# A schedule searched anew: halved first loads, wide filler matmuls and another list of steps

## The chip, the cores and the metric

The kernel runs on one core of a Trainium2 chip. Its time is the device time of one execution in microseconds. Three runs of the kernel before took 821.39, 821.52 and 822.88 us, so the median is 821.52 us; the profiled execution took 821.7 us. The engines are TensorE (PE, with PEld for its weight loads), VectorE (DVE), ScalarE (ACT), GpSimd (POOL) and SyncE (SP), which issues most transfers.

## The reference, cut to what matters

Three stages follow one another on 2304 tokens (4 sequences of 576) with 512 features (8 heads of 64):

```python
kv  = einsum('bhsd,bhse->bhde', k, v)          # linear attention, per batch and head 64x64
out = einsum('bhsd,bhde->bhse', q, kv)
out = out / sqrt(mean(out*out, -1) + 1e-6) * g_norm      # per head
x   = out as (2304, 512)
xn  = x / sqrt(mean(x*x, -1) + 1e-6) * rms_g
x   = (silu(xn @ w_gate) * (xn @ w_val)) @ w_out         # 512 -> 1536 -> 512
h   = x @ w_in
out = where(h > 0, h, exp(min(h, 0)) - 1) @ w_out2       # 512 -> 2048 -> 512
```

The weights arrive in 64 bits and are turned into 32-bit numbers on the chip.

## The kernel before, in words

The tokens lie in 18 tiles of 128. A batch of 576 tokens is four and a half tiles, so tile 4 is shared by batches 0 and 1, and tile 13 by batches 2 and 3. For each batch `sum_kv` (L933) adds up the products of k and v over its tiles in one PSUM bank (step `kv`), `keep_kv` (L954) copies the sum to SBUF on ACT (`kept`), and `attend` (L972) multiplies the queries of a tile with it (`po`). The queries of two tiles come in one load (q0 for tiles 0 and 1, q1 for 2 and 3, q2 for 4 and 5). Behind `po` stand, for every tile, a square on ACT, a mean and a guard on DVE, a power on POOL, two multiplications on DVE, a second square on ACT, a power on POOL and a scaling on ACT (`norm2`). `turn` (`pt`, L1036) transposes two tiles on PE, and ACT and DVE split the result into two parts, xh and xl (L1048, L1046).

The feed-forward stages multiply in three products of such parts (high by high, high by low, low by high). Each weight block has to be converted first (`conversion`, L1079): about six steps on DVE and two on ACT give a high part `h_` and a low part `l_`. The names g0, v0, o0 are the first blocks of w_gate, w_val and w_out; i and p are those of the last stage. Block 0 of tokens (tiles 0 and 1) is multiplied first: `hid_0_0` needs xh and xl of these tiles and g0 and v0; `b_0_0` and `b_0_1` need the gated result (`act`) and o0. Partial sums of the second products are copied to SBUF by ACT (`part`) and added in memory by transfers from POOL.

What stands where is written out in advance. Every piece of work is a step with an engine, an assumed length, predecessors and the buffers it takes. The method `order` (L77) chooses the buffers by a greedy pass over ranks that a table SHIFTS alters; the table ORDER then gives the order in which the instructions of all engines are written. Loads go through SP in one queue. Where the list expects PE to wait between two steps, `run` (L154) puts in filler matmuls of 128 columns (`keep_warm`, L925); they write to an unused part of the bank of the running `kv` sum, so outside such a sum there are none. Ahead of everything PE runs 14 matmuls of 128 columns on zeros (`idle`, L876). Both kinds are in 32-bit floats, and the trace shows two records for one such matmul of 128 columns.

Of the kernel before, what the change touches and what calls it, by code (L numbers as in the profile page):

```python
# [20 lines left out]
WARM = 16  # L21
# [3 lines left out]
class Plan:  # L25
# [6 lines left out]
    PATIENCE = 0.03  # L32
# [25 lines left out]
    def lag(self, e, engine):  # L58
        return self.LAG[e][0] if e == engine else self.LAG[e][1] + self.into.get(engine, 0.0)

    def room(self, kind, engine, chosen):

        best = None
        for slot in self.kinds[kind]:
            if slot in chosen:
                continue
            key = self.holder.get(slot)
            at = 0.0
            if key is not None:
                if any(u not in self.ends for u in self.users[key]):  # L70
                    continue
                at = max((self.reach(u, engine) for u in self.users[key]), default=0.0)
            if best is None or at < best[0]:
                best = at, slot
        return best

    def order(self):  # L77
        self.holder, self.where = dict(self.held), {}
        self.ends, self.log, self.rooms = {}, [], []
        self.clock = dict(self.start)  # L80
        waits = {n: len(s["after"]) for n, s in self.steps.items()}
        ready = {e: [] for e in self.clock}
        for n, k in waits.items():
            if not k:
                ready[self.steps[n]["engine"]].append((n, 0.0))
        left = len(self.steps)
        while left:
            best = None
            for engine, names in ready.items():
                now = self.clock[engine]  # L90
                here = None
                for n, at in names:
                    s = self.steps[n]
                    at = max(now, at)
                    if here and at > here[0] + self.PATIENCE:
                        continue
                    slots = []
                    for kind, key in s["takes"]:
                        r = self.room(kind, engine, [x for x, _ in slots])
                        if r is None:  # L100
                            break
                        at = max(at, r[0])
                        slots.append((r[1], key))
                    if len(slots) < len(s["takes"]):
                        continue
                    if here is None or at < here[0] - self.PATIENCE or (
                        at <= here[0] + self.PATIENCE and (s["rank"], at) < (here[1], here[0])
                    ):
                        here = at, s["rank"], n, slots
                if here and (best is None or here[:2] < best[:2]):  # L110
                    best = here
            if best is None:
                return None
            at, _, n, slots = best
            s = self.steps[n]
            engine = s["engine"]
            for slot, key in slots:
                if slot in self.holder:
                    self.rooms.append((self.holder[slot], n))
                self.holder[slot] = key  # L120
                self.where[key] = slot
            ready[engine] = [x for x in ready[engine] if x[0] != n]
            self.ends[n] = at + s["length"] + s["lat"]
            self.clock[engine] = at + s["length"]
            self.log.append((at, n, engine, s["length"]))
            for x in self.then.get(n, ()):
                waits[x] -= 1
                if not waits[x]:
                    e = self.steps[x]["engine"]
                    ready[e].append((x, max(self.reach(y, e) for y in self.steps[x]["after"])))  # L130
            left -= 1
        return max(self.ends.values())

    def timed(self):

        after = {n: list(s["after"]) for n, s in self.steps.items()}
        for key, taker in self.rooms:
            after[taker] += self.users[key]
        names = list(self.steps)
        assert sorted(ORDER) == list(range(len(names)))  # L140
        self.ends, self.log = {}, []
        self.clock = dict(self.start)
        for i in ORDER:
            n = names[i]
            s = self.steps[n]
            engine = s["engine"]
            at = max([self.clock[engine] if engine != "NOTE" else 0.0] + [self.reach(x, engine) for x in after[n]])
            self.ends[n] = at + s["length"] + s["lat"]
            self.clock[engine] = at + s["length"]
            self.log.append((at, n, engine, s["length"]))  # L150
# [3 lines left out]
    def run(self):  # L154
        self.held, self.start = dict(self.holder), dict(self.clock)
        self.then = {}
        for n, s in self.steps.items():
            for x in s["after"]:
                assert x in self.steps, (n, x)
                self.then.setdefault(x, []).append(n)  # L160
        for n, s in self.steps.items():
            unit = str(n[0] if isinstance(n[0], tuple) else n[:4]).replace(" ", "")
            s["rank"] += SHIFTS.get(unit, 0)
        self.into = {}
        assert self.order(), "no step can start"
        self.into = self.INTO
        self.timed()
        last, end = 0.0, self.steps[self.filled_until]
        for at, n, e, length in self.log:
            call = self.steps[n]["call"]  # L170
            if e == "PE":
                if call and end and last:
                    for _ in range(int((at - last - self.SPACE) / self.FILL)):
                        self.filler()
                last = at + length
                end = end if n != self.filled_until else None
            if call:
                call()


SHIFTS = {
# [625 lines left out]
def linear_attention__swiglu__elu_kernel(  # L807
# [341 lines left out]
    def load(n):  # L1149
        raw_sb[n] = stage(weight[n].bitcast(U32), ("raw", n))  # L1150
# [1034 lines left out]
```

## Time and profile before

| what | value |
|---|---|
| median of three runs | 821.52 us (821.39 to 822.88) |
| profiled execution | 821.7 us, span 819.9 us, so 1.8 us lie around the span |
| mean granted TensorE clock | 0.996 |
| PE, DVE, ACT, POOL busy | 99%, 91%, 78%, 28% |
| memory traffic | 57.2 MB read, 66.1 MB written |

The span runs from the first to the last instruction. An idle time of PE is only seen where no matmul runs; the views used below are the engines' busy time by stretch with the granted clock (1.00 is 2.4 GHz, 0.50 is 1.2 GHz), the waits, and the instructions in order of time.

### The profile page before, as it was taken

Reading aid. Unit: us, or ns where it says so; the run is one execution under the profiler, and the core shown is the slowest. Engines: PE = TensorE matmul, PEld = TensorE weight load, DVE = VectorE, ACT = ScalarE, POOL = GpSimd, SP = SyncE. Lnnn points to the kernel's source line nnn. Section 1 sums busy time; section 2 is a strip of 40 time slices with the busy share of each in tenths; the row PEclk is TensorE's granted clock in tenths of the full one; section 3 lists DMA queues with packets and bytes.
Section 4 is the critical chain, followed back from the end, with each engine's and each line's share of the span. In section 5 each row is a group of like instructions: output and inputs, shape, how many; then the busy total and the mean of one; then the engine's idle time right before and its main releaser. Section 6 shows DMA issues by size and latency. Waiting matters only on the chain.

```text
span 819.9 us, 12523 instructions
## 1 busy us (share of the span) xinstructions
PE 809.4 (99%) x4228; PEld 683.8 (83%) x4228; DVE 747.7 (91%) x1360; ACT 636.7 (78%) x1209; POOL 230.8 (28%) x258
## 2 busy tenths in 40 slices
PE   8999999999999999999999999999999999999997
PEld 7888888888888888888888888888888888888886
DVE  3999999998787888888999999999999999999895
ACT  2789777777677676667655789999999999999891
POOL 3556222123223213113300000123333334233332
PEclk9899999999999999999999999999999999999999
DMA  9953468558657748648972242789989998989989
GB/s 363 354 172 101 119 124 164 125 104 150 132 104 141 131 100 138 121 91 136 159 193 78 78 151 87 183 129 145 158 161 174 155 170 137 182 154 141 124 176 249
DMA packets 56144, 124.06 MB, mean 151 GB/s; under 512 B 6160, under 2 KB 10000, under 8 KB 56080
## 3 DMA queue, kind: packets, MB, share of 16 engines
q0 software_dynamic: 30944, 54.01, 47.4%
q1 hardware_dynamic: 25136, 69.25, 24.6%
q8 instruction: 33, 0.54, 0.3%
q14 instruction: 31, 0.25, 0.1%
HBM read 57.18 MB, written 66.06 MB: 150 GB/s over the span
## 4 chain that ended last, share of the span: by engine, by line
PE 97%; DMA 2%; SPq 0%; DVE 0%; issue 0%
PE b L1362 11%; PE hid L1520 7%; PE hid_g L1520 3%; PE hid_v L1520 3%; PE b L1347 2%; PE po L981 2%; DMA wacc<-in_q 1%; PE pt L1036 1%; DMA wxl<-in_q 1%; PE kv L943 1%; PE ('pu', 0, 10, 3)_a L1231 1%; PE ('pu', 0, 4, 1)_a L1231 1%; PE ('pb', 10, 1)_a L1699 1%; PE ('pu', 0, 11, 3)_a L1231 1%; PE ('pu', 0, 7, 3)_a L1231 1%; PE ('pb', 4, 3)_a L1699 1%
## 5 line engine op out<-in xcount | busy, mean ns | idle before, releaser
L1756 POOL DMA_DIRECT2D out<-part x104 | 91.8, 910 | 163.4 <-DVE part L1723 62.7
L1756 POOL DMA_DIRECT2D mid<-part x64 | 57.0, 1037 | 187.4 <-ACT part L1733 79.9
L1428 ACT ACTIVATE part<-b 128x512 f32<-128x512 f32 x66 | 38.9, 596 | 10.5 <-PE b L1362 3.9
L1434 POOL DMA_DIRECT2D out<-part x12 | 11.0, 917 | 125.4 <-DMA out<-part 107.7
L1565 ACT ACTIVATE e<-e 128x512 f32<-128x512 f32 (+1 forms) x73 | 45.1, 625 | 0.9
L1434 POOL DMA_DIRECT2D mid<-part x26 | 27.7, 1152 | 59.1 <-ACT part L1428 57.0
L1362 PE MATMUL b<-act,h_o 128*128 128x512 f32 x128 | 39.7, 392 | 0.0
L1663 DVE TENSOR_TENSOR e<-e,e 128x512 f32<-128x512 f32 x56 | 38.4, 686 | 0.5
L1001 POOL TENSOR_TENSOR ri<-ms,nhalf 128x8 f32<-128x8 f32 x18 | 32.7, 1818 | 11.8 <-DVE ms L997 11.7
L1362 PEld LDWEIGHTS b<-act,h_o 128*128 128x128 f32 x128 | 23.6, 188 | 4.8 <-issue 0.2
L1362 PE MATMUL b<-act,l_o 128*128 128x512 f32 x64 | 24.9, 389 | 0.0
L1362 PE MATMUL b<-h_p,act 128*128 128x512 f32 (+1 forms) x68 | 23.1, 378 | 0.5 <-DVE far L1468 0.5
L1487 DVE TENSOR_TENSOR far<-far,b 128x512 f32<-128x512 f32 x27 | 18.0, 683 | 5.3 <-PE b L1362 5.1
L1362 PE MATMUL b<-act,h_p 128*128 128x512 f32 x64 | 19.8, 390 | 0.0
L1048 ACT ACTIVATE xh<-pt,gains_sb 128x256 fp32r<-128x256 f32 x36 | 15.7, 480 | 3.8 <-PE pt L1036 3.8
L1347 PE MATMUL b<-act,h_o 128*128 128x256 f32 x96 | 18.2, 285 | 0.0
L1520 PE MATMUL hid<-xh,l_i 128*128 128x256 f32 x64 | 18.1, 283 | 0.0
L1520 PE MATMUL hid<-xl,h_i 128*128 128x256 f32 x64 | 18.1, 283 | 0.0
L1520 PE MATMUL hid<-xh,h_i 128*128 128x256 f32 x64 | 17.9, 280 | 0.0
L1347 PEld LDWEIGHTS b<-act,h_o 128*128 128x128 f32 x96 | 15.9, 190 | 1.3
L1046 DVE SCALAR_TENSOR_TENSOR xl<-pt,gains_sb,xh 128x256 fp32r<-128x256 f32 x36 | 15.9, 476 | 1.1 <-ACT xh L1048 1.1
L1019 POOL TENSOR_TENSOR ri<-ms,nhalf 128x1 f32<-128x1 f32 x18 | 11.0, 615 | 19.0 <-ACT junk L1015 18.9
(2362 smaller groups left out, 3183.8 us busy)
## 6 DMA issues: line engine op xcount, KB each, us to landing
out<-part POOLq DMA_DIRECT2D x116, 256.0 KB, 5.3
mid<-part POOLq DMA_DIRECT2D x90, 256.0 KB, 5.4
raw_i<-in_w_in SPq DMA_DIRECT2D x16, 512.0 KB, 5.0
raw_p<-in_w_out SPq DMA_DIRECT2D x16, 512.0 KB, 5.5
raw_g<-in_w_gate SPq DMA_DIRECT2D x12, 512.0 KB, 5.4
raw_v<-in_w_val SPq DMA_DIRECT2D x12, 512.0 KB, 4.5
raw_o<-in_w_out SPq DMA_DIRECT2D x12, 512.0 KB, 4.8
mid<-part SPq DMA_DIRECT2D x18, 256.0 KB, 2.2
```

What stands on the lines that cost most here:

```text
L981: nc.tensor.matmul(po[r:r1, p * P:(p + 1) * P], qt[:, p, r:r1], kv_sb[b][:, p, :], start=True, stop=True)
L1001: nc.gpsimd.tensor_tensor(ri, ms_t.pop(i), nhalf, op=ALU.pow)
L1231: nc.tensor.matmul(pbank[unit, b], l[:, sl], r, start=first and c == 0 and i == 0, stop=c == 1 and i == 2, skip_group_check=True,)
L1347: nc.tensor.matmul(po[:, j * n:(j + 1) * n], l[:, s], r, start=first and i == j == 0, stop=f == fs[-1] and i == 2, skip_group_check=True,)
L1362: nc.tensor.matmul(po, l, r, start=first and i == 0 and not half, stop=f == fs[-1] and i == 2, skip_group_check=seeded(ph, k, t) or half i ...
L1428: nc.scalar.activation(x, pbank["b", k, t, e][:, :n], AF.Copy)
L1434: nc.gpsimd.dma_start(out=where(ph, t, e), in_=flat(live.pop(key), t or ph), accum_op=ALU.add)
L1487: nc.vector.tensor_tensor(x, x, pbank["b", k, t, e][:, :n], op=ALU.add)
L1520: nc.tensor.matmul(pbank[key][:, j * n:(j + 1) * n], l, r, start=bool(opens) and i == 0, stop=c == KD - 1 and i == 2, skip_group_check=not ...
L1565: nc.scalar.activation(live[key], live[key], AF.Exp, scale=-1.0)
L1663: nc.vector.tensor_tensor(raw(*into), raw(*x), raw(*y), op=ALU.subtract)
L1756: lambda key=key, t=t, e=e: nc.gpsimd.dma_start(out=where(ph, t, e), in_=live.pop(key), accum_op=ALU.add),
```

## The change

1. **Shared tile and first queries in halves.** Tile 4 is packed on the host so that the half of batch 0 (`4a`) and that of batch 1 (`4b`) are each 512 columns over all 128 partitions, and each is a load of its own. q0 is loaded as `q0a` and `q0b`, one for each of its tiles.
2. **Loads reordered.** SP issued 0, 1, 2, 3, 4, q0, gains, g0, q1, 5, 6, 7, 8, v0, q2, o0, q3, q4, 9 and now issues 0, 1, 2, 3, 4a, g0, gains, q0a, q0b, q1, v0, 6, 4b, 5, 7, 8, q2, o0, 9, q3, 10, 12, 11, 13, 16, 14, 15, g1, q4, 17, q5.
3. **Fillers.** One filler matmul has up to 512 columns; where no `kv` sum is open it writes to the bank that the step behind it will take. The matmuls on zeros at the start are 5 of 512 columns.
4. **List searched anew.** SHIFTS and the greedy pass are gone; ORDER and a new table PLACES (the buffer for each take) are written out. The assumed times of the loads and of PE's start differ, and the steps `whole` wait for both of the last tiles' powers.

```diff
-WARM = 16
+WARM = 5
...
-                    for _ in range(int((at - last - self.SPACE) / self.FILL)):
-                        self.filler()
+                    self.filler(n, int((at - last - self.SPACE) / self.FILL))
...
-SHIFTS = {
-    "('go',0)": -166, "('in',0)": -1299, "('go',1)": -9, "('in',1)": -385, "('go',2)": 8, "('in',4)": 28,
...
+PLACES = (
...
-WHOLE_AFTER = 17
+WHOLE_AFTER = 16, 17
...
-    for j in range(WARM - 2):
-        nc.tensor.matmul(idle[:, :P], blank, blank, start=True, stop=True)
+    for j in range(WARM):
+        nc.tensor.matmul(idle, blank, blank.unsqueeze(1).to_broadcast([P, 4, P]), start=True, stop=True)
...
-    def load_kv_tile(i):
-        in_sb[i] = home(i)
-        nc.sync.dma_start(out=in_sb[i], in_=kv[i].rearrange("t j e -> t (j e)"))
+    def load_kv_tile(i, part=None):
+        if i not in in_sb:
+            in_sb[i] = home(i)
+        cs = slice(0, 2 * DM) if part is None else slice(part * DM, (part + 1) * DM)
+        nc.sync.dma_start(out=in_sb[i][:, cs], in_=kv[i][:, cs])
...
-    def keep_warm():
-        if spot:
-            nc.tensor.matmul(spot[0], ident, ident, start=False, stop=False, skip_group_check=True)
+    def keep_warm(n, times):
+        taken = [key for _, key in plan.steps[n]["takes"]]
+        if times > 0 and not spot and taken:
+            own = ps.tile([P, 512], F32, tag=plan.where[taken[0]], name="_".join(map(str, ("warm", *n))))
+        most = 2 if spot else 4
+        while times > 0 and (spot or taken):
+            k = min(times, most)
+            wide = ident.unsqueeze(1).to_broadcast([P, k, P])
+            if spot:
+                nc.tensor.matmul(spot[0][:, :k * P], ident, wide, start=False, stop=False, skip_group_check=True)
+            else:
+                nc.tensor.matmul(own[:, :k * P], ident, wide, start=True, stop=True)
+            times -= k
...
+            if packed:
+                r0 = h % 2 * D
+                r1 = r0 + D
+                at = part * DM + h // 2 * D
+                to = at + HALF
...
-    LOADS = [0, 1, 2, 3, 4, 'q0', 'gains', 'g0', 'q1', 5, 6, 7, 8, 'v0', 'q2', 'o0', 'q3', 'q4', 9, 10, 11, 12, 13, 'q5', 'q6', 14, 15, 16, 17, 'g1', 'v1', 'q7', 'o1', 'q8']
+    LOADS = [0, 1, 2, 3, '4a', 'q0a', 'q0b', 'gains', 'g0', '4b', 'q1', 5, 6, 7, 8, 'v0', 'q2', 'o0', 'q3', 'q4', 9, 10, 11, 12, 13, 'q5', 'q6', 14, 15, 16, 17, 'g1', 'v1', 'q7', 'o1', 'q8']
...
-    plan.clock["DMA"], plan.clock["PE"] = 3.85, 6.75
+    plan.clock["DMA"], plan.clock["PE"] = 2.5, 6.1
...
+    cut = s // P
+    cut_rows = arrays["kv"][cut].reshape(2, d, 2, h // 2, 2, d)
+    arrays["kv"][cut] = cut_rows.transpose(4, 1, 0, 2, 3, 5).reshape(P, 2 * dm)
```

On PE, from the last products of batch 0 to the queries of tile 4 (`po_297` before, `po_308` after), this stood before; `wxl` and `wacc` are the buffers of the loaded tiles and queries, and `kv_105` is the kept sum of batch 0:

```order
L943 MATMUL kv_116<-wacc_142 64x64 x8
L981 MATMUL po_170<-kv_105,wxl_153 128x128 x4
L981 MATMUL po_179<-kv_105,wxl_153 128x128 x4
L943 MATMUL kv_191<-wacc_142 64x64 x8
L981 MATMUL po_200<-kv_105,wacc_175 128x128 x4
L981 MATMUL po_215<-kv_105,wacc_175 128x128 x4
L943 MATMUL kv_191<-wacc_188 64x64 x16
L943 MATMUL kv_191<-wacc_224 64x64 x8
L927 MATMUL kv_191<-ident 128x128
L943 MATMUL kv_191<-wacc_224 64x64 x8
L981 MATMUL po_297<-kv_105,wacc_175 64x128 x4
L981 MATMUL po_297<-kv_106,wacc_175 64x128 x4
```

Before there is one filler here, and none directly ahead of the queries of tile 4. Now the same engine has, from behind the queries of tile 3 (`po_201`) to those of tile 4:

```order
L537 MATMUL warm_kv_4_224<-ident 128x512
L537 MATMUL warm_kv_4_224<-ident 128x128
L562 MATMUL kv_227<-wacc_134 64x64 x8
L535 MATMUL kv_227<-ident 128x256
L535 MATMUL kv_227<-ident 128x128
L562 MATMUL kv_227<-wacc_206 64x64 x16
L562 MATMUL kv_227<-wacc_238 64x64 x8
L535 MATMUL kv_227<-ident 128x128
L562 MATMUL kv_227<-wacc_238 64x64 x8
L537 MATMUL warm_po_306<-ident 128x512
L602 MATMUL po_308<-kv_96,wacc_174 64x128 x4
L602 MATMUL po_308<-kv_97,wacc_174 64x128 x4
```

The products of tile 4 for batch 1 moved behind the queries of tiles 2 and 3, and fillers of 1664 columns in all stand here, 512 of them directly ahead of the queries of tile 4.

On DVE, at the place where o0 becomes ready for `b_0_0` (`l_o` is its low part, `act` the gated result), this stood before:

```order
L1115 TENSOR_SCALAR c_o_351<-raw_o_288 128x512
L1544 TENSOR_TENSOR sa_0_424<-sa_0_424,hid_0_0_362 128x256
L1118 ISA w_o_399<-w_o_399,c_o_351 128x1024
L997 TENSOR_SCALAR ms_411<-ms_411 128x8
L994 TENSOR_REDUCE ms_472<-z_67 128x8
L1305 TENSOR_TENSOR act_0_0_0_431<-sa_0_424,act_0_0_0_431 128x256
L1004 TENSOR_TENSOR z_71<-po_297,ri_422 128x512
L1127 SCALAR_TENSOR_TENSOR l_o_477<-w_o_399,h_o_458 128x512
```

And this stands there now:

```order
L736 TENSOR_SCALAR c_o_323<-raw_o_296 128x512
L618 TENSOR_SCALAR ms_393<-ms_393 128x8
L739 ISA w_o_409<-w_o_409,c_o_323 128x1024
L618 TENSOR_SCALAR ms_422<-ms_422 128x8
L1165 TENSOR_TENSOR sa_0_436<-sa_0_436,hid_0_0_385 128x256
L625 TENSOR_TENSOR z_71<-po_308,ri_414 128x512
L748 SCALAR_TENSOR_TENSOR l_o_471<-w_o_409,h_o_451 128x512
L926 TENSOR_TENSOR act_0_0_0_473<-sa_0_436,act_0_0_0_473 128x256
```

From the first step of g0 to the last row here DVE has the same steps in both lists, but for one guard more after the change; within the list, g0's six steps now come before the first mean, and `l_v`, the low part of v0, before the first `xl`.

## Rows read from the trace of the kernel before

**Rows 1.** The page, part 1: busy us (share of the span) xinstructions of each engine.

```profile
PE 809.4 (99%) x4228; PEld 683.8 (83%) x4228; DVE 747.7 (91%) x1360; ACT 636.7 (78%) x1209; POOL 230.8 (28%) x258
```

**Rows 2.** Stretches: us, busy us (instructions) by engine, granted clock, DMA share, GB/s.

```profile
10.83:20.50 9.67, 7.52 (x115) 6.67 (x114) 7.29 (x18) 3.69 (x8) 5.13 (x4) 1.00 1.03 412
20.50:21.48 0.98, 0.04 (x2) 0.00 (x0) 0.98 (x4) 0.90 (x4) 0.86 (x1) 1.00 1.02 405
21.48:22.42 0.94, 0.00 (x0) 0.00 (x1) 0.94 (x4) 0.93 (x4) 0.94 (x1) 0.50 1.03 414
22.42:28.30 5.88, 5.88 (x31) 5.55 (x32) 5.34 (x12) 3.48 (x8) 1.58 (x3) 0.50 1.03 407
28.30:36.15 7.85, 7.85 (x123) 7.35 (x123) 7.85 (x19) 6.35 (x15) 4.50 (x4) 1.00 0.75 284
36.15:814.40 778.25, 778.25 (x3850) 655.77 (x3848) 724.25 (x1308) 619.84 (x1173) 215.90 (x232) 1.00 0.72 142
814.40:819.90 5.50, 0.84 (x5) 0.44 (x4) 0.84 (x2) 0.00 (x0) 0.00 (x0) 1.00 0.53 197
```

**Rows 3.** PE in order of time: start, us, instruction, count, [idle before, its releaser].

```profile
1.04 4.99 PE L876 MATMUL idle<-z 128*128 128x128 f32 x28 [1.04 <-DVE z L873]
...
9.51 0.49 PE L927 MATMUL kv<-ident 128*128 128x128 f32 x2
10.15 0.68 PE L943 MATMUL kv<-wacc 64*64 64x64 f32 x16 [0.15 <-DMA wacc<-in_kv]
11.81 2.02 PE L981 MATMUL po<-kv,wxl 128*128 128x128 f32 x16 [0.98 <-ACT kv L957]
...
18.58 0.69 PE L943 MATMUL kv<-wacc 128*64 128x64 f32 x16 [0.56 <-DMA wacc<-in_kv]
19.20 0.49 PE L927 MATMUL kv<-ident 128*128 128x128 f32 x2
19.85 0.69 PE L943 MATMUL kv<-wacc 128*64 128x64 f32 x16 [0.17 <-DMA wacc<-in_kv]
22.42 2.88 PE L981 MATMUL po<-kv,wacc 128*64 128x128 f32 x16 [1.89 <-DMA wacc<-in_q]
...
36.15 0.48 PE L1347 MATMUL b<-act,h_o 128*128 128x256 f32 x2
```

**Rows 4.** DVE in order of time, first conversion of g0 to the low part of o0.

```profile
12.86 0.43 DVE L1092 TENSOR_SCALAR c_g<-raw_g 128x512 uint32<-128x512 uint32 x1 [11.87 <-DMA raw_g<-in_w_gate]
13.33 0.43 DVE L1099 TENSOR_SCALAR c_g<-c_g 128x512 f32<-128x512 f32 x1
13.67 0.68 DVE L994 TENSOR_REDUCE ms<-z 128x8 f32<-128x512 f32 x1
...
16.71 0.69 DVE L994 TENSOR_REDUCE ms<-z 128x8 f32<-128x512 f32 x1 [0.31 <-ACT z L990]
...
27.26 0.48 DVE L1046 SCALAR_TENSOR_TENSOR xl<-pt,gains_sb,xh 128x256 fp32r<-128x256 f32 x1 [0.51 <-ACT xh L1048]
...
35.44 0.68 DVE L1127 SCALAR_TENSOR_TENSOR l_o<-w_o,h_o 128x512 fp32r<-128x512 f32 x1
```

**Rows 5.** ACT in order of time: the splitting of tiles 0 and 1.

```profile
26.39 1.69 ACT L1048 ACTIVATE xh<-pt,gains_sb 128x256 fp32r<-128x256 f32 x4 [1.53 <-PE pt L1036]
```

**Rows 6.** Waits: engine, line, waited for: us in total, times, longest us.

```profile
ACT part L1428 <- DMA mid<-part: 3.1, 2, 1.9
ACT part L1719 <- DMA out<-part: 2.8, 1, 2.8
PE b L1362 <- DVE far L1468: 0.5, 1, 0.5
```

**Rows 7.** Transfers by line: engine, count, KB each, median us from issue to landing.

```profile
out<-part POOLq DMA_DIRECT2D x116, 256.0 KB, 5.3
far<-mid SPq DMA_DIRECT2D x18, 256.0 KB, 2.9
wacc<-in_kv SPq DMA_DIRECT2D x7, 512.0 KB, 9.7
```

More of the change, by code (lines that the diff above doesn't have):

```diff
@@ L31 @@
     INTO = {"PE": 0.11, "POOL": 0.1}
-    PATIENCE = 0.03
     def __init__(self, kinds):
@@ L58, in lag @@
     def lag(self, e, engine):
[L59 to L132, printed above, removed]
@@ L134, in timed @@
+        return self.LAG[e][0] if e == engine else self.LAG[e][1] + self.INTO.get(engine, 0.0)
     def timed(self):
[L136 to L139, printed above, removed]
+        names, places = list(self.steps), iter(PLACES)
         assert sorted(ORDER) == list(range(len(names)))
-        self.ends, self.log = {}, []
-        self.clock = dict(self.start)
+        self.ends, self.log, self.rooms, self.where = {}, [], [], {}
@@ L143, in timed @@
+        holder, clock = dict(self.holder), dict(self.clock)
         for i in ORDER:
@@ L145, in timed @@
             s = self.steps[n]
-            engine = s["engine"]
-            at = max([self.clock[engine] if engine != "NOTE" else 0.0] + [self.reach(x, engine) for x in after[n]])
+            engine, after = s["engine"], list(s["after"])
+            for kind, key in s["takes"]:
+                slot = self.kinds[kind][next(places)]
+                if slot in holder:
+                    after += self.users[holder[slot]]
+                    self.rooms.append((holder[slot], n))
+                holder[slot], self.where[key] = key, slot
+            at = max([clock[engine] if engine != "NOTE" else 0.0] + [self.reach(x, engine) for x in after])
             self.ends[n] = at + s["length"] + s["lat"]
-            self.clock[engine] = at + s["length"]
+            clock[engine] = at + s["length"]
             self.log.append((at, n, engine, s["length"]))
@@ L154, in run @@
     def run(self):
[L155 to L166, printed above, removed]
         self.timed()
@@ L841, in linear_attention__swiglu__elu_kernel @@
     PAIRS = (1, 2), (3, 4)
+    halves = (seq // P,)
     const = ctx.enter_context(tc.tile_pool(name="const", bufs=1))
@@ L935, in sum_kv @@
         tiles = tiles_of_batch(b)
+        packed = i in halves
+        part = int(i == tiles[0])
         if i == tiles[0]:
             both = bank(("kv", b))
-            kv_acc[b], spot[:] = both[:, :HALF], [both[:, HALF:HALF + P]]
+            kv_acc[b], spot[:] = both[:, :HALF], [both[:, HALF:]]
             kv_last[:] = [kv_acc[b]]
@@ L942, in sum_kv @@
             s = slice(h % 2 * D, (h % 2 + 1) * D)
+            at, to = h * D, DM + h * D
+            if packed:
[3 more added lines that the diff above has]
+                to = at + HALF
             nc.tensor.matmul(
                 kv_acc[b][s, h // 2 * D:(h // 2 + 1) * D],
-                in_sb[i][r0:r1, h * D:(h + 1) * D],
-                in_sb[i][r0:r1, DM + h * D:DM + (h + 1) * D],
+                in_sb[i][r0:r1, at:at + D],
+                in_sb[i][r0:r1, to:to + D],
                 start=(i == tiles[0] and h < 2),
@@ L957, in keep_kv, with load_q @@
         nc.scalar.activation(t[s, :, s], kv_acc[b][s].rearrange("p (a e) -> p a e", a=KD), AF.Copy)
-    def load_q(j):
+    def load_q(j, part=None):
         src = q[j].rearrange("d j a t -> d (j a t)")
         if f"q{j}" in homes:
-            q_sb[j] = home(f"q{j}")
-            nc.sync.dma_start(out=q_sb[j], in_=src)
+            if j not in q_sb:
+                q_sb[j] = home(f"q{j}")
+            cs = slice(0, 2 * DM) if part is None else slice(part * DM, (part + 1) * DM)
+            nc.sync.dma_start(out=q_sb[j][:, cs], in_=src[:, cs])
         else:
@@ L1820, in linear_attention__swiglu__elu_kernel @@
         LOADS += [f"i{f + j}" for j in range(G)] + [f"p{f + j}" for j in range(G)]
-    plan.clock["DMA"], plan.clock["PE"] = 3.85, 6.75
+    plan.clock["DMA"], plan.clock["PE"] = 2.5, 6.1
+    base = lambda x: int(x.strip("qab")) if isinstance(x, str) else x
+    side = lambda x: "ab".index(x[-1]) if isinstance(x, str) and x[-1] in "ab" else None
     for k, x in enumerate(LOADS):
-        is_q = isinstance(x, str) and x[0] == "q"
         is_w = x in weight
-        takes = [("st0" if is_q or x in early_w else "st", ("raw", x) if is_w else ("q", int(x[1:])))] if is_w or (is_q and x not in homes) else []
-        fn = (lambda x=x: load(x)) if is_w else (lambda x=x: load_q(int(x[1:]))) if is_q else (lambda x=x: load_kv_tile(x))
-        fn = load_gains if x == "gains" else fn
-        late = LOAD if is_w and x not in early_w else 2.0 * (k > LOADS.index("q3"))
-        plan.add(("go", x), "DMA", 0.1 if x == "gains" else 1.27, k, fn, [("go", LOADS[k - 1])] if k else [], takes)
+        is_q = not is_w and isinstance(x, str) and x[0] == "q"
+        takes = [("st0" if is_q or x in early_w else "st", ("raw", x) if is_w else ("q", base(x)))] if is_w or (is_q and x not in homes and side(x) is None) else []
+        fn = load_gains if x == "gains" else (lambda x=x: load(x)) if is_w else (lambda x=x: load_q(base(x), side(x))) if is_q else (lambda x=x: load_kv_tile(base(x), side(x)))
+        late = LOAD if is_w and x not in early_w else 2.0 * (k > LOADS.index("q4"))
+        length = 0.17 if x == "gains" else 1.33 if side(x) is None else 0.67
+        plan.add(("go", x), "DMA", length + (1.2 if k == 2 else 0.0), k, fn, [("go", LOADS[k - 1])] if 0 < k < 4 else [("go", LOADS[3])] if k else [], takes)
         plan.add(("in", x), "NOTE", 0.0, k, None, [("go", x)], lat=0.1 + late)
@@ L1838, in linear_attention__swiglu__elu_kernel @@
                 ("kv", b, i), "PE", KV if seq % P == 0 or i not in cut else 0.5, 50 + 20 * b + 2 * tiles[0], lambda b=b, i=i: sum_kv(b, i),
-                [("in", i)] + ([("kv", b, i - 1)] if i > tiles[0] else []), [("g0", ("kv", b))] if i == tiles[0] else [],
+                [("in", f"{i}{'ba'[i == tiles[-1]]}" if i in halves else i)] + ([("kv", b, i - 1)] if i > tiles[0] else []), [("g0", ("kv", b))] if i == tiles[0] else [],
             )
@@ L1862, in linear_attention__swiglu__elu_kernel @@
         old = [("turn", (i - Z) // 2, half) for half in range(2)] if i >= Z else []
-        plan.add(("po", i), "PE", PO if len(bs) == 1 else 1.9 * PO, r, lambda i=i: attend(i), [("in", f"q{p}"), *kept, *old], [("o0", ("po", i))])
+        plan.add(("po", i), "PE", PO if len(bs) == 1 else 1.9 * PO, r, lambda i=i: attend(i), [("in", f"q{p}{'ab'[i % 2]}" if p == 0 else f"q{p}"), *kept, *old], [("o0", ("po", i))])
         plan.frees(("po", i), [("norm", i)])
@@ L2045, in linear_attention__swiglu__elu_kernel @@
                     plan.add(
-                        ("whole", t, k), "DVE", EW, rank + 10 * c + 2 * o - 1, lambda t=t, k=k: whole(t, k), xold(t, k) + [("invert2", WHOLE_AFTER)],
+                        ("whole", t, k), "DVE", EW, rank + 10 * c + 2 * o - 1, lambda t=t, k=k: whole(t, k), xold(t, k) + [("invert2", i) for i in WHOLE_AFTER],
                         [("U", ("wx", t, k))],
@@ L2159 @@
         "q": rows(q).reshape(nt // 2, 2, P, kd, P).transpose(0, 4, 1, 3, 2),
-        "kv": np.stack([rows(k), rows(v)], axis=2),
+        "kv": np.stack([rows(k), rows(v)], axis=2).reshape(nt, P, 2 * dm),
         "gains": np.concatenate([np.broadcast_to(g_norm, (P, d)), moe_rms_g.reshape(kd, P).T], axis=1),
```

2 lines of the change are left out of this document (1 added, 1 removed), and 901 rows, old and new, of tables (ORDER, PLACES, SHIFTS).

## Prediction

> **What bounds the kernel now.** Read the busy shares first: PE is at 99%, so only the few microseconds in which it does not run useful matmuls at full clock can be won [rows 1]. The stretches show where these lie. From 36.15 to 814.40 us PE is busy without a gap at clock 1.00, 778.25 of 778.25 us [rows 2]; nothing in the list between can be shortened by removing a wait of PE, because it shows none, and the number of useful matmuls does not change. What is left is the start and the end. At the end, PE waits 0.5 us for a sum on DVE in the middle of its last tile, and then the last sum and store follow [rows 2, 6]; the changed list has the same two halves in the same order there, so I cost the end at nothing.
>
> At the start PE lives on loads. They stream: the tiles that PE takes at 18.58 and 19.85 lie 1.27 us apart, which is the price of one load of 512 KB [rows 3], with the DMA engines full [rows 2]. After tile 8 PE has nothing to do until q2 lands at 22.42 [rows 3]. In that gap the granted clock falls from 1.00 to 0.50, at 21.48, and stays there until 28.30 [rows 2]: PE does 5.88 us of work at half speed. At full clock this takes 2.94 us, so 2.94 us is what the fall costs, if all else follows.
>
> All else is DVE. `b_0_0` starts at 36.15; the low part of o0 that it needs is made from 35.44 to 36.12 [rows 3, 4]. So at 36.15 PE does not come late, DVE does. Between the first step of g0 (12.86) and 36.12 DVE idles 0.31 and 0.51 us; 23.26 minus 0.82 leaves 22.4 us of work [rows 4].
>
> **The change part by part.**
>
> *Load order and halves.* q2 has the same loads ahead of it as before (0 to 8, q0, q1, g0, v0, gains), so it lands at 22.4 again. Two loads become four of half size. I take no cost for that, since the queue is full and transfers overlap (9.7 us from issue to landing against 1.27 us apart [rows 3, 7]). From below: no gain, as the bytes are the same. From above: a lone 256 KB read lands in 2.9 us [rows 7]; if the four halves did not overlap at all, they would take 11.6 us instead of 2 times 1.27, and q2 would be 9.1 us late. SP has more issues, but it is 5 to 10 us ahead of the landings. I take the near row, 1.27 per full load. The Trainium skill ("DMA: Bandwidth & Descriptors", "Anatomy of one DMA — SWDGE (gpsimd) path") gives every transfer a fixed 2.0 us beside its bytes, which speaks against halving; two transfers more would by that, unhidden, be an estimated 4 us on q2. The 1.27 us between whole loads in this trace speak against charging it, since the page's own sum for 512 KB is an estimated 3.2 us.
>
> g0 moves from behind 0 to 4, q0 and gains to behind 0 to 3 and 4a: one and a half loads earlier, 1.9 us, so DVE starts at about 10.9 instead of 12.86 [rows 4]. The price: the first queries wait for q0a, which lands behind g0, at about 12.2 instead of 11.81 [rows 3]. It is hidden, as the queries of tiles 2 and 3 wait for q1 anyway and everything from there to 22.4 has gaps.
>
> *Products of tile 4.* The same matmuls of the same shape; nothing either way, bounded by 0.1 us, as 16 records take 0.68 us [rows 3].
>
> *Fillers.* 28 records took 4.99 us at the start [rows 3]; now it is the work of 40, so PE takes up the first tile at about 7.1 us instead of 6.1. That is hidden behind the loads of tiles 3 and 4 (PE still waits for tile 4 at 10.15 [rows 3]); without that cover it would cost 1 us. A filler of 128 columns costs 0.2 us (two records start within 0.49 [rows 3]); those ahead of q2 are four, 0.85 us. Tile 8 comes one load later than before, since v0 is now ahead of it: at 21.1, done at 21.6, filler until 22.5. So the queries of tile 4 start at 22.5, 0.1 late. In exchange PE's longest idle between 10 and 22.5 is, by these landings, 0.7 us ahead of q0a, 0.35 ahead of tile 7 and 0.55 ahead of tile 8. Before, 0.98 us of idle ahead of 11.81 did not lower the clock [rows 2, 3]; 1.89 did. I take the clock as held: gain on PE 2.94 minus 0.1. PE could reach `b_0_0` at 33.3.
>
> *The list up to `b_0_0`.* What is late next is DVE. It has the same work ahead of that place, 22.4 us, and starts at 10.9: 33.3 if it never waits. It will wait: g0's steps now follow one another directly, and a dependent one starts 0.47 after the last instead of 0.34 [rows 4], some 0.4 us in all; 0.2 for the high part of g0 from ACT; and 0.5 behind xh, as in the trace [rows 4], for ACT splits the tiles in 1.69 us and DVE follows [rows 5]. That is 1.1, so `l_o` and `act` are done at 34.4 and `b_0_0` starts at 34.5 instead of 36.15: a lead of 1.65. Bounds: 2.85 (DVE never waits, PE sets it) and 0 (DVE waits as much as it leads). I choose 1.65, because each of the three waits has a row.
>
> *The list behind it.* The steps `whole` wait for one power more; POOL is 28% busy [rows 1] and ORDER sets their place, so I take nothing, and rival 3's price at most. PE has no gap there before, so a lead can be kept or lost but not grow. I take it as kept: the conversions that follow are on a DVE that leads by the same 1.6 us.
>
> Sum against the profiled execution: 821.7 − 1.65 = 820.05. The median of the runs is 0.18 below that execution, so the forecast for the median is 819.9.
>
> **The rivals.** What a measurement of this kernel can tell from no change is about 0.2%, 1.64 us; faster means below 819.88, slower above 823.16.
>
> 1. *DVE or ACT eats the lead.* The clock is held, PE arrives early and waits longer at `xl` or `b_0_0`. For it: DVE is busy 7.85 of 7.85 us from 28.30 to 36.15 [rows 2]. Against it: it starts two microseconds earlier with the same work. Lead 0 to 0.8, about 821.1.
> 2. *The clock falls anyway.* Between tile 4b and q2 PE still idles a fifth of the time, and the fall at 21.48 came when it had been idle only 0.98 us and had done little since 18.58 [rows 2, 3]. Against it: 7.52 busy of 9.67 us was enough before [rows 2]. Then PE again loses the 2.94, and the time is 821.6.
> 3. *Slower: a copy on ACT waits for an accumulating write.* The buffers of the partial sums are dealt out anew by PLACES. A copy into one whose write is still under way stops ACT, the PSUM bank stays full, and PE stands. A write takes 5.3 us to land [rows 7]; ACT met such waits of 3.1 (two) and 2.8 us before without PE feeling it [rows 6]. One that PE feels whole gives 819.9 + 5.3 = 825.2; one felt half 822.6. It decides the sign from 1.65 us on. Against it: the pattern of steps is the same, and PE met none in 778 us.
> 4. *The halves do not overlap.* q2 then lands at 31.5 at worst, 9.1 late, and 821.7 + 9.1 − 2.94 − 0.18 gives 827.7. Against it are the 1.27 us between loads [rows 3]. By the fixed cost that the Trainium skill states (same page and section) q2 would be an estimated 4 us late instead, which makes an estimated 822.6.
>
> That the change does not do what it says would be rival 2.
>
> **How the numbers follow.** Forecast (lead 0.8 to 2.85, 818.7 to 820.7): 0.70, a little under three fifths of it below 819.88. Rival 1: 0.11. Rival 2: 0.06. Rival 3: 0.11, of which 0.08 is above 823.16. Rival 4: 0.02. So faster 0.41 (0.70 × 0.58), slower 0.10, and the same 0.49. The range 818.7 to 821.8 takes in the forecast and rivals 1 and 2; what it leaves out is rivals 3 and 4 and a few hundredths.
>
> **What would show it.** Right: the granted clock is 1.00 from 20 to 30 us; the queries of tile 4 start at 22.4 to 22.7; DVE's first conversion step starts near 10.9; `b_0_0` starts near 34.5 with a short wait of PE for DVE ahead of it; PE has no gap from there to the end, and the last matmul is as far from the end as before. Wrong: a clock of 0.50 behind 21 us (rival 2), `b_0_0` at 35.4 or later at full clock (rival 1), any idle of PE between 40 and 800 us (rival 3), or q2 landing after 23 us (rival 4). A start of `b_0_0` before 33.3 would mean that work had moved ahead of q2, which I do not see in the list.

## The result, and the profile after

The change makes the kernel slower. The changed kernel takes 827.87 us (median of 6 runs, 827.10 to 830.07), the kernel before 821.94 us (6 runs); the ratio is 1.0073 (95% interval 1.0058 to 1.0087). The forecast was 819.9 us with a range up to 821.8, so even the sign was missed. The profiled execution took 827.15 us with a span of 825.4.

The stretches of the changed kernel (us, busy us and instructions of PE, PEld, DVE, ACT and POOL, granted clock, DMA share, GB/s) answer to [rows 2]:

```profile
10.83:20.50 9.67, 9.35 (x110) 7.53 (x108) 8.16 (x18) 4.28 (x9) 4.48 (x4) 1.00 1.03 414
20.50:22.42 1.92, 1.85 (x40) 1.52 (x36) 1.89 (x4) 0.23 (x1) 1.92 (x2) 1.00 1.03 410
22.42:28.30 5.88, 5.61 (x46) 4.30 (x47) 5.78 (x13) 5.84 (x15) 3.18 (x4) 1.00 1.04 411
...
532.80:536.12 3.32, 0.39 (x2) 0.00 (x0) 0.09 (x2) 1.14 (x3) 0.18 (x1) 1.00 0.60 141
536.12:540.20 4.08, 4.08 (x11) 3.22 (x12) 3.87 (x7) 3.66 (x8) 0.68 (x1) 0.58 0.74 124
540.20:820.77 280.57, 280.06 (x1303) 233.79 (x1303) 265.06 (x470) 250.74 (x471) 97.99 (x112) 1.00 0.93 160
```

The start does what it says in this execution: the clock stays at 1.00 where it was 0.50 before. The loss is in the middle. PE does 0.39 us of work in 3.32 us, and in the 4.08 us behind that the granted clock is 0.58 on average.

PE at the start, in order of time (start, us, instruction, count, [idle before, its releaser]), for [rows 3]:

```profile
1.05 6.17 PE L475 MATMUL idle<-z 128*128 128x512 f32 x10 [1.05 <-DVE z L472]
7.27 1.15 PE L562 MATMUL kv<-wxh 128*64 128x64 f32 x32
...
11.24 1.56 PE L537 MATMUL warm_po<-ident 128*128 128x512 f32 x4
13.06 2.02 PE L602 MATMUL po<-kv,wxl 128*128 128x128 f32 x16 [0.26 <-PE warm_po L537]
...
22.19 1.12 PE L537 MATMUL warm_po<-ident 128*128 128x512 f32 x2
23.38 1.58 PE L602 MATMUL po<-kv,wacc 128*64 128x128 f32 x16
...
27.09 1.16 PE L602 MATMUL po<-kv,q 128*128 128x128 f32 x8 [0.21 <-DVE z L625]
...
35.17 0.51 PE L968 MATMUL b<-act,h_o 128*128 128x256 f32 x2
```

`b_0_0` starts at 35.17 instead of 36.15: a lead of 0.98 us, not 1.65. That is one execution of each. In four other profiles of kernels with this same start, all among the experiments below, `b_0_0` starts between 35.68 and 36.65. DVE in the same stretch, for [rows 4]:

```profile
10.39 0.43 DVE L713 TENSOR_SCALAR c_g<-raw_g 128x512 uint32<-128x512 uint32 x1 [9.40 <-DMA raw_g<-in_w_gate]
10.86 0.43 DVE L720 TENSOR_SCALAR c_g<-c_g 128x512 f32<-128x512 f32 x1
...
14.86 0.69 DVE L615 TENSOR_REDUCE ms<-z 128x8 f32<-128x512 f32 x1 [1.20 <-ACT z L611]
...
34.77 0.42 DVE L926 TENSOR_TENSOR act<-sa,act 128x256 fp32r<-128x256 f32 x1
```

DVE's last step for `b_0_0` ends at 35.19, and PE has no gap from 27.09 to 35.17. The two meet there, so this profile does not say which of them set the time.

From `b_0_0` to the end of the span the kernel before took 819.9 − 36.15 = 783.75 us, and the changed one 825.4 − 35.17 = 790.23: 6.48 us more. The chain that ended last shows most of it (start, us, what; SPq is SP's queue, ACTq ACT's sequencer):

```profile
525.67 0.57 ACT c_i L734
526.24 0.02 issue
526.26 0.34 SPq L515
526.60 0.05 issue
526.65 0.48 SPq L1370
527.13 0.05 issue
527.18 7.72 DMA out<-part
...
534.98 0.13 ACT part L1354
535.11 0.36 issue
535.48 0.60 ACT ('pu', 1, 2, 3)_u L886
536.08 0.04 issue
536.12 2.37 PE ('pu', 1, 2, 3)_a L852 x6
```

Read it from the top. SP wants to load the weight block p4 (L515), but the buffer still holds i4, which ACT reads last in `c_i`. So SP stands until 526.26. Behind that load in SP's queue are two writes of partial sums (L1370). The second is 7_4_0, whose data ACT had copied by 521.05 (520.46 + 0.59, the first row below). It goes out at 527.18, 6.1 us late. Beside that load of 512 KB and an accumulating write that POOL issued at 526.03, it takes 7.72 us to land. ACT's next copy into its buffer waits for the landing:

```profile
520.46 0.59 ACT L1340 ACTIVATE part<-('pb', 7, 3)_a 128x512 f32<-128x512 f32 x1
...
530.98 0.60 ACT L1183 ACTIVATE e<-('pu', 1, 2, 3)_b 128x512 f32<-128x512 f32 x1
534.98 0.60 ACT L1354 ACTIVATE part<-('pb', 8, 1)_b 128x512 f32<-128x512 f32 x1 [3.40 <-DMA out<-part]
535.48 0.59 ACT L886 ACTIVATE ('pu', 1, 2, 3)_u<-('pu', 1, 2, 3)_a 128x512 f32<-128x512 f32 x1
```

The copy that PE needs, `pu..._u` at 535.48, is queued behind the waiting one. ACT came for the buffer at 531.58 (534.98 − 3.40). By an estimate from these rows, it took both to stop it, a late write and a slow landing. Gone out as late but landed in 2.0 us (the median of SP's 18 such writes), the write would have been through at 529.2; gone out when SP came free, at 522.40, but landed in 7.72 us, at 530.1.

So ACT's 3.40 us become 2.93 us of idle PE, 3.1 us from matmul to matmul. The low clock behind it costs another 1.7: eleven matmuls of 512 columns, 0.227 us each at full clock, take 4.21 us from 536.12 to 540.33 instead of 2.50.

A smaller wait stands at 115 us. SP issues a write `mid<-part` (0_3_2) at 109.65 right behind the load of g3; it lands 5.35 us later, and ACT waits 2.40 for its buffer. This write is slow but not late, as its data were ready only at 109.62:

```profile
109.04 0.58 ACT L1049 ACTIVATE part<-b 128x512 f32<-128x512 f32 x1
...
109.65 5.35 DMA mid<-part
```

PE loses about 1.2 us in small gaps from 119 to 130 us.

### The profile page after: what moved, and what is told of

The parts are those of the page before. It is cut to its first block, busy times and chain, and to the rows that moved or that the text cites. A ratio compares the mean times of both kernels' runs of the same rounds, so it can differ in the third digit from the quotient of the medians.

```text
span 825.4 us, 12522 instructions
## 1 busy us (share of the span) xinstructions
PE 815.6 (99%) x4224; PEld 681.9 (83%) x4224; DVE 748.9 (91%) x1360; ACT 635.0 (77%) x1209; POOL 230.5 (28%) x258
## 4 chain that ended last, share of the span: by engine, by line
PE 94%; DMA 2%; DVE 1%; ACT 1%; issue 1%; POOL 0%; SPq 0%; ACTq 0%; DVEq 0%; POOLq 0%
PE b L983 10%; PE hid L1141 7%; PE hid_g L1141 2%; PE b L968 2%; PE hid_v L1141 2%; PE po L602 2%; DMA mid<-part 1%; PE kv L562 1%; DMA out<-part 1%; PE pt L657 1%; PE idle L475 1%; PE ('pu', 1, 0, 3)_a L852 1%; PE ('pu', 0, 4, 3)_a L852 1%; PE ('pu', 1, 10, 3)_a L852 1%; PE ('pu', 0, 7, 3)_a L852 1%; PE ('pb', 9, 1)_a L1320 1%
## 5 line engine op out<-in xcount | busy, mean ns | idle before, releaser
L1377 POOL DMA_DIRECT2D mid<-part x64 | 58.9, 1109 | 172.4 <-DVE part L1344 87.9
L1055 POOL DMA_DIRECT2D mid<-part x26 | 27.6, 1145 | 76.5 <-ACT part L1049 68.0
L983 PEld LDWEIGHTS b<-act,h_o 128*128 128x128 f32 x128 | 23.5, 188 | 5.5 <-ACT part L1049 0.8
L921 ACT ACTIVATE act<-sa 128x256 fp32r<-128x256 f32 (+1 forms) x20 | 10.0, 502 | 7.3 <-DVE sa L1165 7.1
```

What stands on the lines that cost most here:

```text
L983: nc.tensor.matmul(po, l, r, start=first and i == 0 and not half, stop=f == fs[-1] and i == 2, skip_group_check=seeded(ph, k, t) or half i ...
L1055: nc.gpsimd.dma_start(out=where(ph, t, e), in_=flat(live.pop(key), t or ph), accum_op=ALU.add)
L1377: lambda key=key, t=t, e=e: nc.gpsimd.dma_start(out=where(ph, t, e), in_=live.pop(key), accum_op=ALU.add),
```

## The experiments

A "ratio" is that of a kernel's runs to runs of the kernel before on the same chip, with its 95% interval. The times of the kernel before have medians of 821.17 to 821.56 there. Code lines in these kernels differ a little from those above. `landed` is SP's write of a partial sum, `go` a load.

**One write ahead of the load.**

```diff
 SP, order of steps
-go p4, landed 7_3_3, landed 7_4_0
+landed 7_3_3, landed 7_4_0, go p4
```

> The changed kernel with two writes of partial sums (out<-part, 7_3_3 and 7_4_0) put ahead of the load of the weight block p4 in SP's queue; nothing else is moved. Theory (one write that stands behind a waiting load comes 5.5 us late, ACT's copy into the same buffer waits 3.4 us, PE stands 2.9 us, and the clock falls behind it for another 1.9 us): the wait of PE at 533 and the low clock behind it both go, 827.9 - 4.9 = 823.0 (822.5 to 823.5). Rival A (the clock falls there for another reason): only the stall goes, 824.9. Rival B (the buffers are short everywhere in this list, the next copy waits instead): 826.5 to 827.9.

Measured: 823.09 us, ratio 1.0025 (1.0016 to 1.0034). There is no wait of PE near 533 us, and the granted clock is 1.00 from 528 to 545. The writes now land in 2.4 us or less. The time lies in the theory's range, but the kernel before is 0.8 us faster on this chip (821.17), so the differences count: 1.9 us above it instead of 5.9. Two moved steps of 4549 take away 4.0 us. That is less than the theory's 4.9 and more than rival A's 3; rival B falls.

**Three writes ahead of loads.**

```diff
-go g3, ..., landed 0_3_2
+landed 0_3_2, go g3, ...
```

> The same, and the write mid<-part of 0_3_2 put ahead of the load of g3, behind which it went out at 109.65 us though its data were there at 107.3. Theory: ACT's wait of 2.4 us at 115 us goes, and of the 1.2 us that PE loses in small gaps from 119 to 130 us some 0.8 come back: 822.2 (821.7 to 822.8). Rival: PE's gaps there have another cause, and it takes the 823.0 of the run with one place mended.

Measured: 823.27 us, ratio 1.0023 (1.0014 to 1.0033): the rival's number. ACT's waits for `mid<-part` are still 3.0 us in sum, the longest now 1.6, and PE still has gaps of 0.37 and 0.54 us at 120 and 129 us. The wait that the move was to remove is not what made those gaps, and their cause stays open. The expectation is wrong in one point: it has the data of 0_3_2 ready at 107.3, but that was another copy's end, and the right figure is 109.62 (above). So the move could not make the write earlier; ahead of the load it landed in 3.1 us instead of 5.35.

**The changed kernel again.** No edit.

> The changed kernel once more, beside the three that follow. Theory: PE's wait near 533 us and the low clock behind it stand in this trace too, 2.9 us (2 to 4) and 1.9 us, and the time is 5 to 6 us over the kernel before. Rival (the wait was an accident of one execution): no such wait here.

Measured: 827.38 us, ratio 1.0080 (1.0068 to 1.0092). PE waits 2.65 us in the same place. But the clock did not fall this time:

```profile
533.00:538.00 5.00, 2.35 (x11) 1.65 (x10) 2.03 (x4) 1.90 (x4) 0.57 (x1) 1.00 0.68 186
538.00:545.00 7.00, 7.00 (x32) 5.77 (x31) 6.96 (x14) 6.68 (x14) 1.15 (x2) 1.00 0.52 112
```

So the stall is there in both profiles, and the price of the clock behind it in one of them. The mean granted clock of each run tells more. It is 0.995 to 0.998 in ten of the changed kernel's eleven runs, and 0.999 in the one profiled here; with the two writes moved it is 0.999 or 1.000 in nine of eleven runs and 0.998 in two. The mean does not say where a clock fell, but it fits a fall behind the stall in most runs.

**The mechanism put into the kernel before.**

```diff
 kernel before, SP, order of steps
-landed 7_4_1, landed 7_3_3, landed 7_3_2, ..., go p4
+landed 7_3_2, ..., go p4, landed 7_4_1, landed 7_3_3
```

> The kernel before with two of its 4545 steps moved: the writes out<-part of 7_4_1 and 7_3_3 stand behind the load of p4 in SP's queue, as in the changed kernel, instead of ahead of it. Theory: they go out at 528.3 instead of 522, land 5 to 7.7 us later, ACT's copy into the buffer of 7_3_3, due at 530.6, waits 2.5 to 5 us, PE stands 2 to 4.5 us near 533, and the clock falls for 3 to 4 us behind it: 3.5 to 6.5 us slower than the kernel before. Rival A (the old list has slack there): within 1 us of the kernel before. Rival B (the wait comes, but the clock stays at 1.00): 2 to 4 us slower.

Measured: 828.97 us, ratio 1.0094 (1.0081 to 1.0107): 7.6 us slower. SP's queue, ACT, PE and the stretch behind them:

```profile
528.46 0.34 SPq L925 DMA_DIRECT2D raw_p<-in_w_out  x1
528.85 1.93 SPq L1758 DMA_DIRECT2D out<-part  x2
...
536.49 0.60 ACT L1742 ACTIVATE part<-('pb', 8, 1)_b 128x512 f32<-128x512 f32 x1 [5.19 <-DMA out<-part]
...
538.63 0.79 PE L1240 MATMUL ('pu', 1, 2, 3)_a<-xh,Sh_i 128*128 128x512 f32 x1 [4.44 <-ACT ('pu', 1, 2, 3)_u L1274]
...
538.40:545.00 6.60, 6.37 (x17) 5.15 (x18) 4.97 (x9) 4.62 (x10) 0.86 (x1) 0.53 0.62 122
```

The wait is at the long end of what was expected (4.44 us of PE for 4.5), the low clock lasts longer than expected, and the sum lies above the range. In one list two writes were moved out of the load's way, in the other two were moved into it. They are not quite the same two (7_3_3 and 7_4_0, then 7_4_1 and 7_3_3), but in both lists ACT's copy waits for the buffer of one of them, PE waits for ACT, and the time moves by 4 and by 7.6 us. That settles the cause of the largest loss.

**The new start with the old list behind it.**

```diff
 order and buffers
-the changed kernel's list throughout
+the changed kernel's list up to 49 us, behind that the list of the kernel before
```

> The changed kernel's start (loads, halves, fillers, and its list up to 49 us) with the order and the buffers of the kernel before for all steps behind that, four buffers renamed where the two meet. Theory (the start gains 0.98 us up to b_0_0 and the new list behind it loses): 821.9 - 1.0 = 820.9 (820.5 to 821.4), no wait of PE at 533, no fall of the clock. Rival (the start itself costs something that shows later, such as fuller queues): 822 or more.

Measured: 821.42 us, ratio 1.0003 (0.9994 to 1.0012). The middle is mended, and from `b_0_0` to the end it takes 783.5 us, as in the kernel before. But the lead of the start is not there: `b_0_0` starts at 36.35. The matmuls on zeros end later in this execution, and PE then idles only 0.26 us until its first queries:

```profile
1.04 7.33 PE L487 MATMUL idle<-z 128*128 128x512 f32 x10 [1.04 <-DVE z L484]
8.43 1.15 PE L574 MATMUL kv<-wxh 128*64 128x64 f32 x32
...
14.22 2.02 PE L614 MATMUL po<-kv,wxl 128*128 128x128 f32 x16 [0.26 <-PE warm_po L549]
```

**A shorter warm-up.** The kernel of the last run with

```diff
-WARM = 5
+WARM = 3
```

> The kernel with the new start and the old list, but with 3 matmuls of 512 columns on zeros ahead of everything instead of 5. Theory (the longer warm-up and the fillers are not hidden: PE has no idle time from 8.4 to 14.2 us in that trace): the first kv sum starts at 6.0 to 6.6 instead of 7.3 to 8.4, the first queries at 12.2 to 12.8 instead of 13.1 to 14.2, b_0_0 at 34.4 to 35 instead of 35.2 to 36.3, 1 us (0.6 to 1.5) less than with 5. Rival (the loads set PE's pace, as the prediction had it): the first queries at 13.1 or later, and the same time.

Measured: 820.34 us, ratio 0.9991 (0.9983 to 1.0000); by the ratios that is 1.0 us less than with 5. The first sum starts at 6.12 and the first queries at 11.92. So with 5 matmuls the loads did not set PE's pace, and the rival falls. With 3 they do in part: PE waits 0.26 us for a load ahead of 11.92 and 1.28 ahead of 18.09. `b_0_0` at 35.12 lies just behind the theory's band; the time is what it expected. Run once more:

> The kernel with the new start, the old list and 3 matmuls of 512 columns ahead of everything, once more, to narrow its interval (0.9983 to 1.0000). Theory: 0.9985 to 0.9995 again, b_0_0 at 34.8 to 35.3. Rival (the gain was the spread of the start): 0.9995 to 1.001.

Measured: 820.53 us, ratio 0.9991 (0.9982 to 1.0000), `b_0_0` at 34.70. Twice the median is 0.7 us under the kernel before by the ratio, each time with an interval that just reaches 1. It is the fastest version found, well ahead of the changed kernel.

**Old list, wide fillers only.**

```diff
 kernel before
-for _ in range(k): self.filler()
+self.filler(n, min(8, k))     # also in the bank that step n will take, up to 512 columns
```

> The kernel before with one thing changed: fillers of up to 512 columns also where no kv sum is open, in the bank of the step behind them (8 of 128 columns ahead of the queries of tile 4, 4 ahead of those of tile 0). Theory (DVE sets the start of b_0_0, and it starts at 12.86 as before): the clock is 1.00 throughout, b_0_0 starts at 35.4 to 36.2, 821.4 (821.0 to 822.0). Rival (the clock alone sets it): b_0_0 at 33.3 and 819.1.

Measured: 820.97 us, ratio 0.9995 (0.9986 to 1.0005). The clock is 1.00, and `b_0_0` starts at 34.89, earlier than the theory's band and far from the rival's 33.3. DVE takes up g0 at 12.65 and is busy 14.88 of the last 14.89 us ahead of `b_0_0`. It needs 22.2 us, and PE once waits 0.6 us for DVE's `xl`. Here DVE is what sets the time.

**Fillers in sums only.** The new start and old list with

```diff
-taken = [key for _, key in plan.steps[n]["takes"]]
+taken = []
```

> The kernel with the new start and the old list, but with fillers only while a kv sum is open, as before the change. Theory (the fillers in the next step's bank are what holds the clock): the clock is 0.50 from some point between 20 and 23 us to some 28, PE does 5 to 6 us of work at half speed there, b_0_0 starts at 36 to 37 us, 0.3 to 1.5 us slower than with them. Rival (the earlier and wider fillers in the sums hold it): the clock stays at 1.00 and b_0_0 starts about 34.5, because the queries of tile 4 no longer stand behind a filler.

Measured: 820.86 us, ratio 1.0002 (0.9991 to 1.0012), clock 1.00, `b_0_0` at 35.02. The theory misses: with the longer warm-up, the clock holds in the profiled execution without the fillers in the next step's bank. Whether the new order of the loads or the fillers in the sums hold it was not separated, and it need not hold each time: one of the twelve runs has a mean clock of 0.994 and takes 824.74 us. With the shorter warm-up:

> The same with fillers only while a kv sum is open. Theory (DVE sets b_0_0 in both, so 0.9 us of filler ahead of the queries of tile 4 cost nothing): the clock stays at 1.00, b_0_0 at 34.8 to 35.3, and the same ratio as the run beside it, within 0.0008. Rival A (PE sets it): 0.5 us less. Rival B (with the shorter warm-up the idle times ahead of tile 8 grow and the clock falls): b_0_0 at 36 or later and 0.8 us more.

Measured: 820.64 us, ratio 0.9994 (0.9986 to 1.0003), and rival B's mechanism in the trace: PE idles 1.53 us ahead of 12.11 and 1.96 us ahead of 17.99, and the clock falls. `b_0_0` starts at 35.73, not at B's 36 or later. The median is 0.0003 of the time above that of the run beside it, which lies inside the intervals and is less than B's 0.8 us. The fall is probably not in every execution: six of the eleven runs have a mean clock of 1.000, five 0.997 or 0.998. The profiled one fell at 18 us:

```profile
15.50:18.00 2.50, 0.54 (x7) 0.38 (x6) 2.42 (x6) 1.17 (x3) 2.50 (x2) 1.00 1.04 407
18.00:20.00 2.00, 2.00 (x18) 1.75 (x19) 1.97 (x6) 0.72 (x2) 1.71 (x2) 0.51 1.03 410
```

**The old order with halved loads, wide fillers and 3 matmuls on zeros.**

```diff
 kernel before, SP
-go 4, q0, gains, g0, q1
+go 4a, q0a, gains, g0, q0b, 4b, q1
```

> The order and the buffers of the kernel before throughout, DVE's steps of the start among them, with these parts of the change alone: tile 4 and the first queries in halves (SP issues 0 to 3, 4a, q0a, gains, g0, q0b, 4b, q1, and the rest as before), fillers of up to 512 columns also in the next step's bank, and 3 matmuls of 512 columns on zeros at the start. Theory (DVE sets b_0_0: 22.3 us of work from g0's first step in the old order, against 23.8 in the new one, where steps that need one another stand back to back): g0 is taken up at 11.5 to 12.2 instead of 12.7, b_0_0 starts at 34 to 34.6, the list behind takes the 779.4 to 780.2 us that it took in the other runs with it, and the time is 0.9 to 1.6 us under the kernel before (ratio 0.998 to 0.999). Rival (from 35 us on PE or the loads set the start): b_0_0 at 35 or later, ratio 0.9985 or more.

Measured: 821.18 us, ratio 0.9996 (0.9987 to 1.0004). This is the rival's outcome, though the interval reaches into the theory's 0.998 to 0.999. The profile explains little, because the execution was the slowest of eleven (822.79): `b_0_0` is at 36.96, behind waits of PE for loads (0.89, 0.67 and 0.62 us) and for DVE's `xl` (0.89), and of DVE for v0 (1.49) and for ACT (0.84). The gain that was expected is not shown.

**The new list mended, with the shorter warm-up.** The three writes ahead of loads, and WARM = 3.

> The changed kernel with the three writes put ahead of the weight loads, and 3 matmuls of 512 columns at the start instead of 5. Theory (the change loses by the late writes and by the longer warm-up, and by nothing else but the small waits at 120 and 130 us): 1.1 us less than with the three writes alone, which was 1.0023 times the kernel before, so 1.0005 to 1.0015. Rival (the new list loses elsewhere too, and the lead is given back in it): 1.002 or more.

Measured: 821.41 us, ratio 1.0000 (0.9991 to 1.0009), a little better than expected. Three moved steps and two matmuls fewer at the start give back all that the change lost, and the kernel as a whole is level with the kernel before. Behind the same shorter warm-up the old list had 0.9991. The two intervals overlap, so whether the mended new list still loses something is open.

## Why the prediction was wrong

**The step that failed is "the list behind it".** It said that a lead is kept, and took nothing for the new list. In the profiled execution the list lost 6.48 us: 3.1 by PE's wait for ACT's copy, which a late and slow write held up; 1.7 by the clock behind it; some 1.2 by the gaps around 125 us, whose cause is open; the rest was not found. With the two writes ahead of the load, 4.0 us of it are gone. Rival 3 came near the mechanism (a copy on ACT waits for a write, and PE feels it whole) and had 0.11. But it named an accumulating write, which POOL issues, and the one that stopped ACT is a plain write of SP. Its price went by [rows 7], 5.3 us for one landing, 825.2 in sum; it left out that the write may go out late and that the clock may fall behind the stall. That 825.2 lies nearer to 827.87 than the forecast is luck in so far as its terms are others. The argument against it was "the pattern of steps is the same, and PE met none in 778 us". But waits that PE did not feel, as in [rows 6], say nothing of another place: the one of 2.8 us ends at 804.90, while ACT's copy into the buffer of this case ran in the kernel before at 530.62 without a wait. And the pattern was not the same on SP: the kernel before issued the two writes ahead of the load of p4, the new list behind it. The order of SP's queue, which is written out in the list, was not read there.

The Trainium skill ("DMA: Bandwidth & Descriptors", "Issuing engines are not separate DMA queues") says that transfers of all engines interleave on the same DMA engines, and that issuing from several engines at once saves only the sequencer's time, "usually small relative to the DMA itself". The trace agrees with the first half: the late write, beside a weight load, took 7.72 us against the 2.0 us median of the 18 writes `out<-part` that SP issues. It agrees with the second half too, as far as that goes: issuing took SP 0.34 us for the load and 0.48 us for the write. What cost the time is something that the sentence does not speak of, a sequencer that waits: the data of the write were 6.1 us old when SP issued it.

**The start was half right.** By steps:

- *g0 and the clock.* DVE's first step came at 10.39 (predicted 10.9), and the clock was 1.00. Both right. Which part of the change holds the clock is not settled: with the long warm-up it held in one profile without the fillers in the next step's bank. And the 2.94 us were read from one execution of the kernel before. Of its 97 runs beside the experiments, 34 have a mean granted clock of 0.999 or more, and chip by chip their medians are 0.6 to 1.1 us below the others'. The mean does not say where the clock fell, but a fall that costs 2.94 us in every run would not leave this.
- *The warm-up is hidden.* Wrong. It ended at 7.22, as predicted (7.1), but the loads no longer cover it: the first queries came at 13.06 instead of 12.2, DVE waited 1.20 us for their squares, and two matmuls fewer bring 1.0 us. Some 0.8 us of the delay is not the warm-up's but that of the filler at 11.24, to which the prediction gave no cost: the queries start 2.43 us behind the last sum of 4a (10.63), and only 1.66 us behind it (10.84 to 12.50) in the profile with fillers in sums only.
- *q2 and the queries of tile 4.* 23.38 instead of 22.5: the last filler, 1.12 us from 22.19, stands ahead of them. No wait for q2 shows.
- *What sets `b_0_0`.* The prediction read in the kernel before that "PE does not come late, DVE does", because `l_o` is done at 36.12. But PE had no gap there from 22.42 to 36.15 (5.88 busy of 5.88 us, 7.85 of 7.85 [rows 2]), and the chain that ended last runs on PE alone in that stretch. At full clock PE would have been there earlier: DVE bounds what could be won, and is not what PE waited for. That DVE sets the place once the clock holds is shown for the old list with wide fillers; in the changed kernel the two meet.
- *DVE's work.* The term of 22.4 us plus waits of 1.1 was mis-sized. From 10.39 to 35.19 it is 24.8 us: 1.2 of waiting, all of it for ACT behind the late queries, and 23.6 of work. The 0.4 taken for steps that follow one another directly is 1.2: some ten steps now take 0.12 us more each (`c_g` 0.46 us to the next step instead of 0.34). DVE began 0.5 us earlier than predicted and needed 1.3 more than the 23.5, so its last step ends at 35.19, not 34.4.
- *Halves.* Rival 4 did not come: the first queries wait for no load, and tile 4 neither. The 2.0 us that the prediction takes from the Trainium skill stand in a section on transfers that GpSimd issues, while SP issues these loads; no run here shows such a cost in the stream.
- *The end.* Right: PE waits 0.51 us for `far`, as in [rows 6].

## What to carry to other kernels

A queue that is served in order turns one waiting transfer into a delay of all behind it: where a list is rearranged, read each queue for transfers that are ready but stand behind one whose buffer is still in use, and follow who reuses their buffers. A wait that did no harm in one place says nothing of the room in another; ask at each place what stands behind the waiting instruction. Price a stall of PE with the clock that may fall behind it. And before you set out to win a loss that one profile shows, look in the other runs at how often it is there.

## What the runs showed that was not expected

The matmuls on zeros at the start take different times in different executions of the same code. Ten records took 6.17 us in the profile above, and 7.63 when the changed kernel was profiled again:

```profile
1.04 7.63 PE L475 MATMUL idle<-z 128*128 128x512 f32 x10 [1.04 <-DVE z L472]
```

The counts show how: the same ten records, but more of the long kind (duration in ns, shortest, median, longest).

```profile
L475 PE MATMUL idle<-z x10: 592/592/1221, 1.0 to 6.6; 128*128 128x512 f32 x10
L475 PE MATMUL idle<-z x10: 592/1061/1221, 1.0 to 8.1; 128*128 128x512 f32 x10
```

The long ones take about twice as long as the short ones, as at half and at full clock, so the clock probably rose later in the second; these rows do not show why. All that stands behind them on PE moves along, so that `b_0_0` came at 35.17 in the one and at 36.65 in the other. A long warm-up that is not covered therefore costs more in some executions than in others; with 6 records (4.85 us in the second profile of the short warm-up) it was covered better. And a stall of PE did not always lower the clock: it stayed at 1.00 behind 2.65 us, was 0.58 on average over 4.08 us behind 2.93, and 0.53 over 6.60 us behind 4.44. At the start it fell behind 1.96 us with the shorter warm-up and fillers in sums only. So the length of the idle time alone did not decide it.
